# GEGLU feed-forward on one core: the place of ScalarE's Gelu table load, and of one token tile's second product in the down projection

## The chip, the core and the metric

The kernel runs on one core of a Trainium2 chip. TensorE multiplies matrices (PE in the profile, its weight loads are PEld), VectorE (DVE) and ScalarE (ACT) do elementwise work and move results between PSUM and SBUF, GpSimd (POOL) does some elementwise work, and SyncE (SP) issues most DMAs; ScalarE issues a few at the start. The metric is the device time in microseconds (us) of one execution. The five runs before the change gave 272.87 to 273.47 us, with a median of 273.18.

## What is computed

```python
B, S, D, F = 32, 32, 1024, 3584
x: (B, S, D)   w_gate, w_up: (D, F)   w_down: (F, D)      # all bfloat16

def reference(x, w_gate, w_up, w_down):
    return (_gelu(x @ w_gate) * (x @ w_up)) @ w_down      # gelu with the tanh approximation
```

There are 1024 tokens. The hidden tensor has 3584 columns, which is 28 tiles of 128.

## The kernel before

**How the program is written.** Every operation is recorded by one helper (`add`, line 52), so the profile names line 117, where all of them are emitted. Groups are told apart by the tiles that they write and read. TensorE runs its work in the order in which it is recorded. The other engines' operations, DMA issues among them, are sorted by a due time `at` and, where that is equal, by the order of recording (line 88). The due times are constants and running sums of expected matmul times; they order the queues and make nobody wait. Waits come from data: an operation waits for the writers and readers of the cells that it touches. Each engine works through its queue in order, so an operation that waits holds up all that stands behind it on that engine.

**The start (lines 196 to 230, and 247 to 270).** The first four column tiles of the hidden tensor are computed for the first 512 tokens, gate and up, in eight PSUM banks. The contraction over D goes by eight blocks k of 128. For k = 0 and 1, the tokens come in as they are (`xn`) and TensorE transposes them. For k = 2 to 7, they come in by transposing DMAs on SP's queue, the first of which (k = 2) stands behind SP's `xn` and its two gate loads. The weights `first` come in by block: SP loads gate of k = 0 and 1; ScalarE's queue holds half of `xn`, up of k = 0 and 1, then gate and up of k = 2, gate and up of k = 3 (lines 219 to 221), and then a one-column Gelu (line 222, into `warm`). That Gelu makes ScalarE load its table of functions early, long before the first Gelu that counts. All of these have the due time 0, so ScalarE takes them in the order of recording. The weights of k = 4 and 5, and of 6 and 7, also stand on ScalarE's queue, but the first of each waits for matmuls of k = 0 or of k = 1 (lines 264 to 267). After k = 3 the eight banks are copied to SBUF (`kept`).

**The up stage.** The hidden tensor is made with a seven-product block scheme in place of eight products: the two halves of the tokens by pairs of column tiles (p, p + 14), with sums of blocks of x in `S` and sums of weights in `T`. ScalarE and VectorE copy, apply Gelu and multiply, into `hT`.

**The down stage (lines 459 to 588).** The same scheme is used for `hT` times `w_down`: four token tiles t, halves of tokens, of contraction, and of output columns. Products are swept in the order 1, 2, 7, 5, 6, 3, 4 (line 491). A sweep has, for each of four token tiles, 14 matmuls (`NK`) of 512 columns; products 1 and 2 are in bfloat16, straight from `hT` and `w_down`, and the others take sums that VectorE and ScalarE prepare during the sweeps (`prep7` to `prep4`). A sweep accumulates in four PSUM banks, `PA` = 0 to 3 or `PB` = 4 to 7, one for each token tile. After product 1 of a token tile, ScalarE copies the bank of `PA` to one of `PB` (`done1`), since product 1 enters both the first output quarter and the others. Product 2 is then added to `PA`, which completes the output quarter (first tokens, first columns); `done2` copies it to `o11`, from where SP stores it.

One of these 28 sweeps over a token tile is placed differently. Sweep 2 goes over three token tiles only, by `range(5 - n)` on line 509. For the fourth, `done1` makes a second copy of product 1 into an SBUF tile `p1`. After sweep 4, at the very end, `p1` is put back into two banks, as 384 and 128 columns, and product 2 of this token tile is added there: 14 matmuls of 384 columns, then 14 of 128 (lines 578 to 588). ScalarE copies out the first piece and VectorE the second, and SP stores each. The start times `begin[n]` on lines 490 to 494 and the token tile that is held back to the end of the first four contraction steps (`held`, line 504) follow from this placement.

**The end.** Output DMAs have one due time, `end`, so SP takes them in the order of recording. SP then waits until all have landed.

Of the kernel before, what the change touches and what calls it, by code (L numbers as in the profile page):

```python
# [6 lines left out]
P = 128  # L7
BF16 = mybir.dt.bfloat16
FP32 = mybir.dt.float32
# [114 lines left out]
def bass_standalone__geglu_ffn__sampling_kernel(  # L124
# [10 lines left out]
    _, F = w_gate.shape  # L135
# [3 lines left out]
    out_r = of.rearrange("(tc p) d -> p tc d", p=P)  # L139
# [4 lines left out]
    pr = _Program()  # L144

    with ExitStack() as es:
        def sb(name, shape, dtype):
            return es.enter_context(nc.sbuf_tensor(name, shape, dtype))
# [6 lines left out]
        o11 = sb("o11", [P, 4, 512], BF16)  # L155
        ident = sb("ident", [P, P], BF16)
        warm = sb("warm", [P, 2], FP32)
        p1 = sb("p1", [P, 512], FP32)
        ps = es.enter_context(nc.psum_tensor("ps", [P, 8, 512], FP32))
        const0 = nc.const_aps.tensor(0.0, [P, 1], FP32)  # L160

# [3 lines left out]
        wd = [[arena[:, a:a + 7168].rearrange("p (k n) -> p k n", n=512) for a in row] for row in ((0, 7168), (14336, 21504))]  # L165
# [13 lines left out]
        def mm(bank, lhsT, rhs, start, stop, held=False, add=False):  # L179
            return pr.add("pe", held_matmul if held else "matmul", ps[:, bank, 0:rhs.shape[-1]], lhsT, rhs,  # L180
                          start=start, stop=stop, skip_group_check=add)
# [4 lines left out]
        def act(out, a, f, at):  # L186
            return pr.add("act", "activation", out, a, f, at=at)

        def dma(eng, out, a, at, name, after=()):
            return pr.add(eng, "dma_start", out, a, at=at, dma=name, after=after)  # L190

        GELU, COPY = ACTF.Gelu_apprx_tanh, ACTF.Copy
# [14 lines left out]
        def load_first(eng, j, k0, k1, after=()):  # L207
            dma(eng, first[:, j, k0:k1, :], w_r[j][:, k0:k1, 0:4 * P], 0, f"w0_{j}_{k0}", after)
# [10 lines left out]
        for k in range(2, 4):  # L219
            load_first("act", 0, k, k + 1)  # L220
            load_first("act", 1, k, k + 1)
        act(warm[:, 0:1], const0, GELU, 0)
        for k in range(NX):
            for i, b in enumerate((6, 7) if k == 0 else (4, 5)):
                half = ps[:, b, 0:P].bitcast(BF16)
# [22 lines left out]
        bank = lambda b: ps[:, b, :]  # L248
        steps = [(m, j, k) for k in range(DK - KO) for j in range(2) for m in range(4)]
        for m in range(4):  # L250
            steps += [(m, j, k) for j in range(2) for k in range(DK - KO, DK)] + [(m, None, None)]
        for m, j, k in steps:
            if j is None:
                at = 17.0 + m * 0.87
# [80 lines left out]
        def stat(p, j, k):  # L335
            if p in (8, 9):
                return brief[:, j, k, (p % 2) * P:(p % 2 + 1) * P]
            return pair_w(p, 0, slice(k, k + 1))[:, j, 0, :]

        for p in range(4, EARLY):  # L340
            at = 18.9 + (p - 4) * 3.46
# [23 lines left out]
        for p in range(NP):  # L365
# [11 lines left out]
            at = lambda s: t0 + s * SLOT  # L377
# [82 lines left out]
        NK = len(KL)  # L460
# [7 lines left out]
        def ht(i, j, k, t):  # L468
            m = (KL if j == 0 else KR)[k]
            return hT[:, m, i * 512 + t * P:i * 512 + (t + 1) * P]  # L470
# [13 lines left out]
        PA, PB = (0, 1, 2, 3), (4, 5, 6, 7)  # L484
# [3 lines left out]
        F, H = 0.2266, 0.216  # L488
        begin = {}
        now = base  # L490
        for n in (1, 2, 7, 5, 6, 3, 4):
            begin[n] = now
            now += (3 if n == 2 else 4) * NK * (H if n < 3 else F)
        end = now + NK * H

        def out_dma(i, t, j, src):
            dma("sp", out_r[:, 4 * i + t, j * 512:(j + 1) * 512], src, end, "out")
# [1 line left out]
        EDGE = 4  # L499

        def sweep(n, banks, start, stat, mov, done, prep=None):


            held = 2 if n == 7 else 3
            steps = [(t, k) for k in range(EDGE) for t in range(4) if t != held] + [(held, k) for k in range(EDGE)]
            steps += [(t, k) for k in range(EDGE, NK - EDGE) for t in range(4)]
            steps += [(t, k) for t in range(4) for k in range(NK - EDGE, NK)]
            if n < 3:
                steps = [(t, k) for t in range(5 - n) for k in range(NK)]
            made = set()  # L510
            for i, (t, k) in enumerate(steps):
                if prep and k // 2 not in made:
                    made.add(k // 2)
                    prep(k)
                mm(banks[t], stat(k, t), mov(k), start and k == 0, k == NK - 1, add=not start)
                if k == NK - 1:
                    done(t, begin[n] + (i + 1) * (H if n < 3 else F))

        def done1(t, at):
            act(bank(PB[t]), bank(PA[t]), COPY, at)  # L520
            if t == 3:
                act(p1[:, :], bank(PA[t]), COPY, at)
        sweep(1, PA, True, lambda k, t: ht(0, 0, k, t), lambda k: wd[0][0][:, k, :], done1)

        def done2(t, at):
            act(o11[:, t, :], bank(PA[t]), COPY, at)
            out_dma(0, t, 0, o11[:, t, :])
        sweep(2, PA, False, lambda k, t: ht(0, 1, k, t), lambda k: wd[1][0][:, k, :], done2)


# [34 lines left out]
        one_t = lambda b: (lambda k, t: S[:, s_at(b, k), t * P:(t + 1) * P])  # L565
        one_w = lambda b: (lambda k: T2r[:, t_at(b, k), :])
        sweep(7, PA, True, one_t(0), one_w(0), lambda t, at: act(p7[t], bank(PA[t]), COPY, at), prep7)
        sweep(5, PA, True, one_t(1), one_w(1), lambda t, at: act(p5[t], bank(PA[t]), COPY, at), prep5)
        sweep(6, PB, False, one_t(2), one_w(2), lambda t, at: act(bank(PA[t]), bank(PB[t]), COPY, at), prep6)
# [4 lines left out]
        sweep(3, PB, False, one_t(2), lambda k: S[:, c_at(0, k), :], done3, prep3)  # L574
        sweep(4, PA, False, lambda k, t: S[:, c_at(1, k), t * P:(t + 1) * P], one_w(2), done4, prep4)


        pieces = ((PB[0], 0, 384), (PB[1], 384, 512))
        for b, c0, c1 in pieces:
            act(ps[:, b, 0:c1 - c0], p1[:, c0:c1], COPY, begin[4] + 6)  # L580
        for b, c0, c1 in pieces:
            for k in range(NK):
                mm(b, ht(0, 1, k, 3), wd[1][0][:, k, c0:c1], False, k == NK - 1, add=True)
            if c0 == 0:
                act(o11[:, 3, c0:c1], ps[:, b, 0:c1 - c0], COPY, end)
            else:
                pr.add("dve", "tensor_copy", o11[:, 3, c0:c1], ps[:, b, 0:c1 - c0], at=end)
            dma("sp", out_r[:, 3, c0:c1], o11[:, 3, c0:c1], end, "out")

        sems, totals = pr.finish(nc, es)  # L590
        with nc.Block() as block:
            for name, e in (("sync", "sp"), ("scalar", "act"), ("gpsimd", "pool"), ("tensor", "pe"), ("vector", "dve")):
# [30 lines left out]
```

## Time and profile before

| | |
|---|---|
| median of five runs | 273.18 us (272.87 to 273.47) |
| the profiled execution | 273.33 us, of which the profile's span is 271.3 us |
| PE busy | 267.9 us, 99% of the span |
| DVE busy | 203.5 us, 75% |
| ACT busy | 132.8 us, 49% |
| POOL busy | 37.1 us, 14% |
| granted TensorE clock | 1.000 over the span |

The page gives each engine's busy time, then the span in 40 slices, the chain of work that ended last, and the costliest groups of instructions. In a group, "out<-in" names the tiles, and the last columns are the busy time, the mean duration of one instruction and the engine's idle time before them. The timeline gives start and length of merged runs of like instructions, in us from the start of the span; a "q" behind an engine's name (ACTq, SPq) is its instruction sequencer, which issues DMAs. Matmuls overlap: one of 512 columns in bfloat16 is shown with 0.38 us, but a new one starts every 0.216 us.

### The profile page before, as it was taken

How to read it: one execution, taken by the hardware profiler on the slowest of the kernel's cores; microseconds unless marked ns; L12 is line 12 of the kernel's file. 1: busy time of each engine (PE TensorE's matmuls, PEld its weight loads, DVE VectorE, ACT ScalarE, POOL GpSimd, SP SyncE). 2: the span in 40 equal slices, each digit the busy share in tenths (PEclk: the TensorE clock that was granted, in tenths of full speed). 3: DMA queues.
4: the chain of work that ended last, by engine and by line, in shares of the span. 5: the costliest groups of instructions: out<-in, count | busy, mean ns of one | idle time of the engine just before them, and what ended most of it. 6: DMA issues, size and time to landing. Idle time of an engine off the chain costs nothing.

```text
span 271.3 us, 3323 instructions
## 1 busy us (share of the span) xinstructions
PE 267.9 (99%) x1206; PEld 191.6 (71%) x1206; DVE 203.5 (75%) x238; ACT 132.8 (49%) x213; POOL 37.1 (14%) x23
## 2 busy tenths in 40 slices
PE   8999999999999999999999999999999999999996
PEld 3444448888888888888776776664458888888884
DVE  1341988898899889988764739289976999999911
ACT  2335777566756675667455564531220305067452
POOL 1000003023302330234345160000000000000000
PEclk9999999999999999999999999999999999999999
DMA  7999970050491500842900070293010000002102
GB/s 180 262 291 197 272 192 4 7 149 0 126 293 48 155 0 2 255 171 66 247 0 0 0 257 16 79 347 118 0 39 19 4 0 0 0 0 80 58 19 97
DMA packets 47039, 27.46 MB, mean 101 GB/s; under 512 B 8624, under 2 KB 47024, under 8 KB 47024
## 3 DMA queue, kind: packets, MB, share of 16 engines
q1 hardware_dynamic: 44800, 25.30, 34.2%
q10 hardware_dynamic: 2224, 1.97, 2.9%
q8 instruction: 9, 0.15, 0.2%
q14 instruction: 6, 0.05, 0.1%
HBM read 23.33 MB, written 2.10 MB: 94 GB/s over the span
## 4 chain that ended last, share of the span: by engine, by line
PE 96%; DMA 2%; SPq 0%; issue 0%; DVE 0%
PE ps L117 96%; DMA arena<-in_x_dram 2%; SPq L117 0%; DVE o L117 0%
## 5 line engine op out<-in xcount | busy, mean ns | idle before, releaser
L117 PE MATMUL ps<-S,T 128*128 128x512 f32 x560 | 129.2, 391 | 0.0
L117 PEld LDWEIGHTS ps<-S,T 128*128 128x128 f32 x560 | 105.1, 188 | 22.4
L117 ACT ACTIVATE tmp<-ps 128x512 f32<-128x512 f32 x64 | 37.9, 594 | 52.2 <-PE ps L117 52.2
L117 POOL TENSOR_TENSOR T<-arena 128x1024 fp32r<-128x1024 bf16 x17 | 36.4, 2151 | 124.6 <-PE ps L117 74.3
L117 PE MATMUL ps<-T,S 128*128 128x512 f32 x224 | 51.3, 390 | 0.0
L117 DVE TENSOR_TENSOR T<-arena,T 128x1024 fp32r<-128x1024 bf16 x42 | 50.9, 1218 | 0.2
L117 PEld LDWEIGHTS ps<-T,S 128*128 128x128 f32 x224 | 42.1, 188 | 8.8
L117 DVE TENSOR_TENSOR hT<-tmp,ps 128x512 bf16<-128x512 f32 x56 | 37.1, 684 | 14.3 <-PE ps L117 11.9
L117 PE MATMUL ps<-arena 128*128 128x512 bf16 x192 | 43.2, 382 | 0.4 <-DMA arena<-in_x_dram 0.3
L117 ACT ACTIVATE ps<-ps 128x512 f32<-128x512 f32 x44 | 25.6, 584 | 36.6 <-PE ps L117 36.6
L117 DVE TENSOR_TENSOR tmp<-ps,tmp 128x512 f32<-128x512 f32 x28 | 19.4, 691 | 23.2 <-PE ps L117 23.2
L117 PEld LDWEIGHTS ps<-arena 128*128 128x128 bf16 x192 | 17.7, 98 | 24.5 <-issue 3.8
L117 DVE TENSOR_TENSOR T<-arena 128x1024 fp32r<-128x1024 bf16 x25 | 30.0, 1218 | 5.0 <-PE ps L117 4.4
L117 PE MATMUL ps<-arena,hT 128*128 128x512 bf16 (+2 forms) x126 | 24.6, 356 | 0.0
L117 DVE TENSOR_TENSOR ps<-ps,tmp 128x512 f32<-128x512 f32 x32 | 22.2, 695 | 3.0 <-PE ps L117 3.0
L117 PEld LDWEIGHTS ps<-arena,hT 128*128 128x128 bf16 x126 | 11.7, 98 | 12.7 <-issue 0.5
L117 ACT ACTIVATE tmp<-tmp 128x512 f32<-128x512 f32 x28 | 17.6, 631 | 2.4 <-DVE tmp L117 2.1
L117 DVE TENSOR_TENSOR S<-hT 128x1024 fp32r<-128x1024 bf16 x14 | 16.6, 1217 | 0.0
L117 ACT ACTIVATE T<-arena 128x1024 fp32r<-128x1024 bf16 x14 | 14.8, 1060 | 0.0
L117 ACT ACTIVATE ps<-hT 128x512 f32<-128x512 f32 x18 | 10.7, 599 | 8.0 <-DVE hT L117 8.0
L117 ACT ACTIVATE hT<-ps 128x512 f32<-128x512 f32 x14 | 8.0, 599 | 10.9 <-PE ps L117 10.9
L117 PE MATMUL ps<-S 128*128 128x512 f32 x56 | 12.9, 389 | 0.0
(32 smaller groups left out, 88.8 us busy)
## 6 DMA issues: line engine op xcount, KB each, us to landing
arena<-in_w_down_dram SPq DMA_DIRECT2D x4, 1792.0 KB, 9.3
arena<-in_w_gate_dram SPq DMA_DIRECT2D x10, 512.0 KB, 3.9
arena<-in_w_up_dram SPq DMA_DIRECT2D x10, 512.0 KB, 6.0
out_dram<-arena SPq DMA_DIRECT2D x12, 128.0 KB, 1.7
arena<-in_w_gate_dram SPq DMA_DIRECT2D x4, 256.0 KB, 5.0
arena<-in_w_up_dram SPq DMA_DIRECT2D x4, 256.0 KB, 5.2
arena<-in_w_up_dram ACTq DMA_DIRECT2D x4, 128.0 KB, 4.8
arena<-in_w_gate_dram ACTq DMA_DIRECT2D x2, 256.0 KB, 5.0
```

The costliest lines, as they stand in the source:

```text
L117: ins = name(eng, *args, **kw) if callable(name) else getattr(eng, name)(*args, **kw)
```

## The change

Two things change. First, the one-column Gelu on `warm` moves forward on ScalarE's queue by two DMA issues: it now stands behind gate and up of k = 2 and ahead of gate and up of k = 3. Second, the late placement of the fourth token tile's product 2 is taken out: sweep 2 covers all four token tiles, `p1`, its copies, the two pieces and their stores are gone, and the fourth token tile of this quarter is copied to `o11` and stored in `done2` as the other three are. The bookkeeping of `begin`, `end` and `held` follows.

```diff
-        p1 = sb("p1", [P, 512], FP32)
...
         for k in range(2, 4):
             load_first("act", 0, k, k + 1)
             load_first("act", 1, k, k + 1)
-        act(warm[:, 0:1], const0, GELU, 0)
+            if k == 2:
+                act(warm[:, 0:1], const0, GELU, 0)
...
         for n in (1, 2, 7, 5, 6, 3, 4):
             begin[n] = now
-            now += (3 if n == 2 else 4) * NK * (H if n < 3 else F)
-        end = now + NK * H
+            now += 4 * NK * (H if n < 3 else F)
+        end = now
...
-            held = 2 if n == 7 else 3
-            steps = [(t, k) for k in range(EDGE) for t in range(4) if t != held] + [(held, k) for k in range(EDGE)]
+            steps = [(t, k) for k in range(EDGE) for t in range(3)] + [(3, k) for k in range(EDGE)]
...
             if n < 3:
-                steps = [(t, k) for t in range(5 - n) for k in range(NK)]
+                steps = [(t, k) for t in range(4) for k in range(NK)]
...
-        def done1(t, at):
-            act(bank(PB[t]), bank(PA[t]), COPY, at)
-            if t == 3:
-                act(p1[:, :], bank(PA[t]), COPY, at)
-        sweep(1, PA, True, lambda k, t: ht(0, 0, k, t), lambda k: wd[0][0][:, k, :], done1)
+        sweep(1, PA, True, lambda k, t: ht(0, 0, k, t), lambda k: wd[0][0][:, k, :],
+              lambda t, at: act(bank(PB[t]), bank(PA[t]), COPY, at))
...
-        pieces = ((PB[0], 0, 384), (PB[1], 384, 512))
-        for b, c0, c1 in pieces:
-            act(ps[:, b, 0:c1 - c0], p1[:, c0:c1], COPY, begin[4] + 6)
-        for b, c0, c1 in pieces:
-            for k in range(NK):
-                mm(b, ht(0, 1, k, 3), wd[1][0][:, k, c0:c1], False, k == NK - 1, add=True)
-            if c0 == 0:
-                act(o11[:, 3, c0:c1], ps[:, b, 0:c1 - c0], COPY, end)
-            else:
-                pr.add("dve", "tensor_copy", o11[:, 3, c0:c1], ps[:, b, 0:c1 - c0], at=end)
-            dma("sp", out_r[:, 3, c0:c1], o11[:, 3, c0:c1], end, "out")
```

## The prediction

> **What bounds the kernel now.** I read the page's busy times first, then the chain that ended last, then the timelines of both ends, because the change touches the first 12 us and the last sweeps.
>
> ```profile
> span 271.3 us, 3323 instructions
> PE 267.9 (99%) x1206; PEld 191.6 (71%) x1206; DVE 203.5 (75%) x238; ACT 132.8 (49%) x213; POOL 37.1 (14%) x23
> PE 96%; DMA 2%; SPq 0%; issue 0%; DVE 0%
> ```
>
> TensorE is busy all the time. So only three things can move the end: TensorE's own work, a hole in its stream, and what comes before its first or after its last matmul. The chain in order of time shows them:
>
> ```profile
> 2.22 6.62 DMA arena<-in_x_dram
> ...
> 8.97 260.11 PE ps L117 x1174
> ...
> 269.11 0.29 DVE o L117
> ```
>
> The one wait at the front is for a transposing DMA of x, the slice of k = 2, issued at 2.22. From 8.97 on, TensorE never waits until VectorE's last copy. TensorE's timeline gives the prices:
>
> ```profile
> 4.61 4.03 PE L117 MATMUL ps<-arena 128*128 128x512 bf16 x16
> 8.97 13.40 PE L117 MATMUL ps<-arena 128*128 128x512 bf16 x61 [0.33 <-DMA arena<-in_x_dram]
> ...
> 181.19 21.32 PE L117 MATMUL ps<-arena,hT 128*128 128x512 bf16 x98
> 202.17 38.44 PE L117 MATMUL ps<-T,S 128*128 128x512 f32 x168
> 240.45 12.86 PE L117 MATMUL ps<-S 128*128 128x512 f32 x56
> 253.14 12.85 PE L117 MATMUL ps<-T,S 128*128 128x512 f32 x56
> 265.84 3.23 PE L117 MATMUL ps<-arena,hT 128*128 128x384 bf16 x28
> ```
>
> The 98 matmuls are sweeps 1 and 2 (56 + 42). They start every (21.32 - 0.38) / 97 = 0.216 us, 0.38 being the length shown of the last one. The last row is the piece that the change removes.
>
> ScalarE's timeline at the start, where each weight load is one row:
>
> ```profile
> 2.28 0.45 ACTq L117 DMA_DIRECT2D arena<-in_w_gate_dram  x1
> 2.76 0.45 ACTq L117 DMA_DIRECT2D arena<-in_w_up_dram  x1
> 3.24 0.45 ACTq L117 DMA_DIRECT2D arena<-in_w_gate_dram  x1
> 3.73 0.47 ACTq L117 DMA_DIRECT2D arena<-in_w_up_dram  x1
> 4.23 1.28 ACT L117 ACT_TABLE_LOAD   x1 [4.23 <-issue]
> 5.52 0.20 ACT L117 ACTIVATE warm<-const-float32-0.0 128x1 f32<-128x1 f32 x1
> 6.95 0.39 ACTq L117 DMA_DIRECT2D arena<-in_w_gate_dram  x1
> ```
>
> **Part 1, the down projection.** *TensorE.* 14 matmuls of 512 columns come into sweep 2: 14 x 0.216 = 3.02 us. All later sweeps move back by that. The last sweep (4) ended at 253.14 + 12.85 = 265.99, so TensorE now ends at 269.01. Before, it ended at 265.84 + 3.23 = 269.07. Gain 0.06.
>
> *The tail behind the last matmul.* Before: VectorE copies 128 columns in 0.29 us and a store of 32 KB lands 1.44 us after issue. After: the last token tile of sweep 4 has an odd number, so ScalarE copies 512 columns and 128 KB are stored. Both stood in the trace already, only not last: that copy ran at 266.03 for 0.60 us, 0.04 behind its matmul, and its store landed in 1.70 us.
>
> ```profile
> 266.03 0.60 ACT L117 ACTIVATE arena<-ps 128x512 bf16<-128x512 f32 x1 [1.22 <-PE ps L117]
> 268.32 0.49 ACT L117 ACTIVATE o<-ps 128x384 bf16<-128x384 f32 x1 [1.69 <-PE ps L117]
> ```
>
> So the copy costs 0.60 - 0.29 = 0.31 more and the store 1.70 - 1.44 = 0.26 more. SP's final wait and the engines' exits follow the landing alike. **Sum of part 1: -0.06 + 0.31 + 0.26 = +0.51 us.** The rows are close copies of what will run, so I allow 0.1 either way.
>
> *What else moves.* Gone from ScalarE: the copy to `p1` (0.59 us) and two copies back (0.47 and 0.26), all beside TensorE's work; gain nothing. Added: one copy to `o11` (0.60 us) at the end of sweep 2. It frees the fourth bank for sweep 7, which holds that token tile back by 12 matmuls (2.7 us), so 2.1 us are spare; without that cover it would cost 0.64. Its store joins SP's queue behind three like it and lands in 1.7 us; the next store behind it is due some 40 us later. VectorE is the risk: it is busy 47.8 of the 51 us from 203 to 254. But it prepared sweep 7 by 201.5 and then stood still for 4.35 us until sweep 7 released a buffer at 205.8. With sweep 7 3.02 us later, that wait is 3.02 longer and all behind it keeps its distance to TensorE, which had no hole there. Due times of `prep3` and `prep4` shift by up to 3.02 too, and VectorE's order stays. Cost nothing; were VectorE to lose one preparation (1.22 us) of its lead, at most that.
>
> **Part 2, the table load.** Nothing is added: 1.28 us of load and 0.20 us of Gelu move ahead of two issues. GpSimd's queue is not touched, and SP's only by the store above. The first Gelu that counts is due at about 17 us, so neither place matters for it. What counts is whether the two issues are held. In the trace's records, VectorE's semaphore instructions in its busiest stretch come about 0.13 us after the start of the instruction before them, not earlier: a sequencer seems to hand over an instruction only as the engine starts it. By that, gate of k = 3 is issued when `warm` starts: 3.24 + 1.28 = about 4.55 in place of 3.24, and up of k = 3 at 5.05 in place of 3.73. The ends are 0 and 1.28 + 0.20 = 1.5 us; I take 1.3.
>
> *Is that late?* Gate landed at 8.58 and was first needed at 8.97 + 8 x 0.216 = 10.70; up landed at 9.78 and was needed at 11.56. Slack 2.12 and 1.78. A shift of 1.3 to 1.5 is covered. The loads behind them wait for k = 0 until 6.95, when ScalarE is free either way (up of k = 3 is issued by 5.7).
>
> *Does anything gain?* The k = 2 slice of x, issued at 2.22, landed at 8.84; 15 of the 16 DMA engines had reported by 8.10, the last 0.74 later, while that engine set was also moving the weights of k = 3 (their packets run from 6.58 to 9.1). Held weights leave that stretch to x. TensorE, from 8.26 on (its sixteenth matmul of k = 0 and 1), could have gone on at 8.48, and went on at 8.97. So the gain lies between 0 and 0.49. Contention could also turn against x, by the loads meeting the later slices instead; k = 3's slice landed at 10.10 for a need at 10.70, so a loss needs 0.6 first. I take 0.30: the laggard near the other engines, not fully.
>
> [...]
>
> **The sum.** +0.51 - 0.30 = +0.2 us. The profiled execution took 273.33, 0.15 above the median, so 273.5 against it, and 273.4 as a median. About 0.2% (0.55 us) is what a measurement of this kernel can tell from no change.
>
> **The rivals.** *A, the issues are not held, or x comes no earlier.* For it: the data of that slice had all started moving by 6.95, and up to 6.57 ScalarE's ring is full of k = 2 whatever happens. Against: the one late DMA engine. It gives +0.51, 273.7, just inside 0.2%.
>
> *B, slower: the weights of k = 3 come late.* Moved back, they stand behind or beside the transposes that SP issues at 3.49 and 4.78. The slowest issue of that time, a transpose at 7.39, took 6.8 us to land. If up of k = 3, issued at 5.2, took that, it would land at 12.0; with x 0.30 earlier it is needed at 11.26, so TensorE stands for 0.74, and the sum is +0.51 - 0.30 + 0.74 = +0.95, 274.1. It decides as soon as up of k = 3 lands over 0.35 late. Against: ScalarE's loads took 4.5 to 6.1 us, and 5.2 + 6.1 = 11.3.
>
> *C, no cost at the end and the full slot at the front.* The stores' landing could be as short as the 1.44 of 32 KB: -0.06 + 0.31 - 0.49 = -0.24, 272.9. Even this isn't faster by 0.2%; that needs 0.3 us more, which no row offers.
>
> **How the numbers follow.** Forecast (x earlier by 0.1 to 0.49, the tail as computed, 273.1 to 273.7): 0.55. A: 0.25. B: 0.12. C: 0.05; something I don't see: 0.03. The range leaves out the far part of B and C and the unseen: 272.95 to 274.05. Slower by over 0.2%: 0.03 of the forecast, four tenths of A as its centre lies 0.04 us from the bound (0.10), nearly all of B (0.11), 0.01 unseen: 0.25. Faster: 0.03. Within 0.2%: 0.72.
>
> **What would show it.** In ScalarE's timeline, the table load should start near 3.2 and gate of k = 3 be issued near 4.55; if it is issued near 3.3, A holds. TensorE's rows at the start should part at 8.5 to 8.8 in place of 8.97, and have no new wait near 10.5 to 11.6 (B). There should be one run of 112 matmuls for sweeps 1 and 2, no hole after it, and the last instruction should be ScalarE's copy of 0.60, with a 128 KB store behind it. A wait of TensorE in sweeps 5 or 6 would mean that VectorE's lead was thinner than I read it.

## The result, and the profile after

The changed kernel takes 273.77 us (median of 33 runs, 273.06 to 274.76); the kernel before, measured beside it, 272.97 (56 runs, 272.27 to 274.25). The ratio is 1.0028 with a 95% interval of 1.0020 to 1.0036: slower by 0.76 us, 0.55 to 0.98. The forecast was 273.4 in a range of 272.95 to 274.05, with +0.2 us against before. The range holds the time, but the loss is larger than forecast, and one term of the sum was wrong.

The page of the changed kernel, then its chain in order of time (start, length, what):

```profile
span 272.0 us, 3290 instructions
PE 268.4 (99%) x1192; PEld 190.9 (70%) x1192; DVE 203.2 (75%) x237; ACT 131.8 (48%) x210; POOL 37.2 (14%) x23
PE 99%; ACT 0%; issue 0%
```

```profile
0.73 0.04 issue
0.78 3.88 PE ps L117 x16
4.66 0.05 issue
4.71 264.51 PE ps L117 x1176
269.22 0.02 issue
269.24 0.60 ACT arena L117
```

The chain no longer passes through a DMA: in this execution TensorE waits for nothing from 4.71 on. And yet the span is longer, 271.96 us in place of 271.27 in the traces' records. TensorE's timeline at both ends:

```profile
4.71 20.65 PE L117 MATMUL ps<-arena 128*128 128x512 bf16 x90
...
181.37 24.35 PE L117 MATMUL ps<-arena,hT 128*128 128x512 bf16 x112
205.36 38.46 PE L117 MATMUL ps<-T,S 128*128 128x512 f32 x168
243.66 12.86 PE L117 MATMUL ps<-S 128*128 128x512 f32 x56
256.35 12.85 PE L117 MATMUL ps<-T,S 128*128 128x512 f32 x56
```

Sweeps 1 and 2 are one run of 112 matmuls, the later sweeps stand unbroken behind it, and sweep 4 ends at 256.35 + 12.85 = 269.20. ScalarE's timeline at the end and at the start:

```profile
269.24 0.60 ACT L117 ACTIVATE arena<-ps 128x512 bf16<-128x512 f32 x1 [1.22 <-PE ps L117]
```

```profile
2.76 0.45 ACTq L117 DMA_DIRECT2D arena<-in_w_up_dram  x1
3.25 1.28 ACT L117 ACT_TABLE_LOAD   x1 [3.25 <-issue]
3.31 0.39 ACTq L117 DMA_DIRECT2D arena<-in_w_gate_dram  x1
3.73 0.48 ACTq L117 DMA_DIRECT2D arena<-in_w_up_dram  x1
4.54 0.20 ACT L117 ACTIVATE warm<-const-float32-0.0 128x1 f32<-128x1 f32 x1
7.62 0.42 ACTq L117 DMA_DIRECT2D arena<-in_w_gate_dram  x1
```

The last lines decide the second half of the change. The table load starts at 3.25 and runs to 4.53, but gate of k = 3 is issued at 3.31, while it runs, and up of k = 3 at 3.73, as before. The one-column Gelu takes its turn on the engine at 4.54, after both. So the issues are not held; the queue goes on past a running table load and past a Gelu that has not begun.

**Where the 0.69 us between the two traces lie.** I cut both at TensorE's first matmul on `S` and `T`, which is the first one of the seven-product scheme: at 40.02 us before and 40.19 after, so the start took 0.17 more. From there to the last matmul it is 228.84 before and 228.63 after, 0.21 less. From the last matmul's start to the span's end it is 2.42 before and 3.15 after, 0.73 more. Together +0.69. The last store is a different one in each; the first row is that of before, the second that of the changed kernel (size, median us from issue to landing):

```profile
out_dram<-o SPq DMA_DIRECT2D x1, 32.0 KB, 1.4
```

```profile
out_dram<-arena SPq DMA_DIRECT2D x12, 128.0 KB, 1.7
```

### The profile page after: what moved, and what is told of

Same layout as the page of the kernel before. It is cut to its first block, busy times and chain, and to the rows that moved or that the text cites. A ratio compares the mean times of both kernels' runs of the same rounds, so it can differ in the third digit from the quotient of the medians.

```text
span 272.0 us, 3290 instructions
## 1 busy us (share of the span) xinstructions
PE 268.4 (99%) x1192; PEld 190.9 (70%) x1192; DVE 203.2 (75%) x237; ACT 131.8 (48%) x210; POOL 37.2 (14%) x23
## 4 chain that ended last, share of the span: by engine, by line
PE 99%; ACT 0%; issue 0%
PE ps L117 99%; ACT arena L117 0%
## 5 line engine op out<-in xcount | busy, mean ns | idle before, releaser
L117 PE MATMUL ps<-arena,hT 128*128 128x512 bf16 x112 | 24.3, 379 | 0.0
L117 PEld LDWEIGHTS ps<-arena,hT 128*128 128x128 bf16 x112 | 10.9, 98 | 13.3 <-issue 0.3
```

Source lines behind the costliest of these rows:

```text
L117: ins = name(eng, *args, **kw) if callable(name) else getattr(eng, name)(*args, **kw)
```

## The experiments

There were two questions: whether the loss comes from the end alone, or whether the moved table load costs something at the start that one trace can't show; and whether the forecast's gain at the start would have come, had the weights really been held. Each ratio is to the kernel before, run beside it. Three kernels, e8_nowarm, e9_half and e10_eighth, were run once each, for their traces alone.

### The table load alone, and the end alone

e1_table, the kernel before with only the first part of the diff:

```diff
-        act(warm[:, 0:1], const0, GELU, 0)
+            if k == 2:
+                act(warm[:, 0:1], const0, GELU, 0)
```

> The kernel before with the table load moved alone; its late product is kept. Theory 1 (the 0.52 us at the end that both traces show is not all: the moved table load makes the start dearer on average): 0.15 to 0.35 us slower than before. Theory 2 (the load doesn't hold the issues, so the start is the same but for chance): within 0.1 us of before. The forecast's own step (the issues are held and x of k = 2 comes earlier): 0.1 to 0.4 us faster. In the profile, the two gate and up issues of k = 3 near 3.31 and 3.73 by theories 1 and 2.

Measured: ratio 1.0004 (0.9988 to 1.0019). ScalarE's timeline has the load at 3.25, the two issues at 3.31 and 3.73 and the Gelu at 4.54, as in the changed kernel. The slices of x landed no earlier (8.94 us for k = 2, against 8.84 before).

e2_tail, the kernel before with only the second part of the diff:

```diff
-            now += (3 if n == 2 else 4) * NK * (H if n < 3 else F)
-        end = now + NK * H
+            now += 4 * NK * (H if n < 3 else F)
+        end = now
...
-        pieces = ((PB[0], 0, 384), (PB[1], 384, 512))
```

> The kernel before with product 2 of the fourth token tile back in its sweep; the table load stays behind k = 3. Theory 1: 0.45 to 0.6 us slower than before, less than the whole change. Theory 2: as slow as the whole change, 0.55 to 0.95 us, which the end alone would then have to give (only 0.52 is in the traces). From the last matmul's start to the end of the span 3.15 us in place of 2.42, by both.

Measured: ratio 1.0009 (0.9994 to 1.0024). The end is as expected, 3.15 us. The whole times of these two kernels can't tell the theories apart: the interval of a ratio over some dozen runs is 0.8 us wide.

### What the whole times can't tell, the records can

Cut at the first matmul on `S` and `T`, the traces fall into two parts of very different kind:

| kernel | product 2 of the fourth tile | first matmul on S and T | from there to the end |
|---|---|---|---|
| before | late, 384 + 128 | 40.02 | 231.25 |
| e1_table | late, 384 + 128 | 40.12 | 231.27 |
| e3_held | late, 384 + 128 | 39.33 | 231.27 |
| e5_held_again | late, 384 + 128 | 39.24 | 231.29 |
| e7_x_first | late, 384 + 128 | 42.25 | 231.24 |
| e11_table_first | late, 384 + 128 | 39.97 | 231.28 |
| after | in sweep 2 | 40.19 | 231.77 |
| e2_tail | in sweep 2 | 39.46 | 231.80 |
| e6_after_held | in sweep 2 | 40.31 | 231.76 |
| e8_nowarm | in sweep 2 | 39.29 | 231.78 |
| e4_whole | late, 512 | 40.82 | 231.82 |
| e9_half | late, 256 + 256 | 39.80 | 231.55 |
| e12_eighth_apart | late, 448 + 64 | 39.67 | 231.62 |
| e10_eighth | late, 448 + 64, with a wait (below) | 40.29 | 233.11 |

The last column repeats to within 0.05 us and depends on the end alone: 231.27 in the mean with the small last piece, 231.78 in the mean of the four with product 2 in its sweep. So the second part of the change costs 0.51 us, shown by ten traces. The column before it moves by 1.5 us (39.29 to 40.82) even without the three held kernels and e7_x_first, among kernels whose early instructions hardly differ. That is the noise of this kernel. Where the table load moved forward without a hold (after, e1_table, e11_table_first) the column has 40.19, 40.12 and 39.97; where it stayed (before, e2_tail, e4_whole, e9_half, e10_eighth, e12_eighth_apart) it has 40.01 in the mean, from 39.46 to 40.82.

### What the end is made of

e4_whole keeps the late place and takes away the small piece:

```diff
-        pieces = ((PB[0], 0, 384), (PB[1], 384, 512))
+        pieces = ((PB[0], 0, 512),)
```

> The kernel before with the late product 2 kept late but in one piece of 512 columns, not 384 and 128. If the gain of the late placement lies only in the small last piece (copy of 0.29 in place of 0.60 us, store of 1.44 in place of 1.70): 0.5 us slower than before, from the last matmul's start to the end of the span about 2.95 us (0.17 less than with an fp32 last matmul). If it lies in the place itself (relief for VectorE or the banks in between): no more than 0.2 us slower.

Measured: ratio 1.0029 (1.0015 to 1.0043), and 231.82 us in the table, as slow as with product 2 in its sweep. From the last matmul to the end it is 3.15, not 2.95 as I wrote, because a bfloat16 matmul of 512 columns, shown with 0.38 us, ends no earlier than the fp32 one with 0.39. The place itself buys nothing; only the small last piece does. ScalarE's last copy in this kernel:

```profile
269.91 0.60 ACT L117 ACTIVATE o<-ps 128x512 bf16<-128x512 f32 x1 [2.44 <-PE ps L117]
```

e9_half, e10_eighth and e12_eighth_apart change the size of the last piece.

```diff
+        pieces = ((PB[0], 0, 256), (PB[1], 256, 512))      # e9_half
+        pieces = ((PB[0], 0, 448), (PB[1], 448, 512))      # e10_eighth
```

> The kernel before with the late product in pieces of 256 and 256 columns in place of 384 and 128. By the forecast's sum of the end: matmuls 14 x 2 x 0.109 = 3.05 us, as before; VectorE's last copy of 256 columns about 0.42 in place of 0.29, by the rows of 128 and 512 columns (0.29, 0.69); the store of 64 KB about 1.50 in place of 1.44; from TensorE's first matmul of k = 4 to the end of the span 259.03 us, 0.2 more than before (258.84). If the size of the last piece doesn't matter and only its being apart does: 258.85.

Measured: 231.55 from the first matmul on `S` and `T`, 0.28 more than with 128 columns (0.2 was expected). The copy took 0.43 and the store 1.56. The size of the last piece is what counts.

```profile
268.93 0.43 DVE L117 CAST o<-ps 128x256 bf16<-128x256 f32 x1 [3.29 <-PE ps L117]
```

> The kernel before with the late product in pieces of 448 and 64 columns. If a matmul of 64 columns starts every 0.028 us, as half of one of 128: the copy takes about 0.23 in place of 0.29 and the store about 1.42, and from k = 4 to the end it is 0.05 to 0.1 us less than before (258.75). If the weight load of 0.1 us sets the pace instead: 14 x 0.03 to 0.07 us more, 0.35 to 0.9 us more than before (259.2 to 259.7).

Measured: matmuls of 64 columns start every 0.029 us, so the weight load (98 ns each in the profile of before) doesn't set the pace. But the end came 1.84 us later than with 128. VectorE's row tells why:

```profile
271.33 0.22 DVE L117 CAST o<-ps 128x64 bf16<-128x64 f32 x1 [5.22 <-DMA out_dram<-o]
```

It waited for the store of the first piece. The program tracks SBUF in cells of 256 bytes; column 448 lies inside a cell that the first piece's store reads. This was a fault of the experiment, so the last 64 columns got a tile of their own:

```diff
+        tip = sb("tip", [P, 64], BF16)
...
-                pr.add("dve", "tensor_copy", o11[:, 3, c0:c1], ps[:, b, 0:c1 - c0], at=end)
+                pr.add("dve", "tensor_copy", tip[:, :], ps[:, b, 0:c1 - c0], at=end)
```

> The kernel before with pieces of 448 and 64 columns again, the last 64 columns now in an SBUF tile of their own, so that VectorE's copy no longer waits for the store of the first piece (in the run before it waited 1.9 us for that). From TensorE's first matmul on S and T to the end of the span: 231.27 us for the kernel before; here the copy 0.22 in place of 0.29, the store 1.41 in place of 1.44, the matmuls 14 x (0.189 + 0.029) = 3.05 as before, so 231.15, 0.1 us less. In the time of whole runs this is below what rounds can tell: ratio 0.998 to 1.001. If the store of the first piece, issued at most 0.5 us earlier, holds up the last one on SP's queue: 0.2 to 0.4 us more than before.

Measured: ratio 1.0002 (0.9988 to 1.0015); 231.62 in the table, 0.35 more than before. The copy did shorten, but the store didn't come earlier, and it took 1.53 us to land in place of 1.44. SP's timeline at the end:

```profile
268.98 0.33 SPq L117 DMA_DIRECT2D out_dram<-o  x1
269.35 0.43 SPq L117 DMA_DIRECT2D out_dram<-tip  x1
```

ScalarE's copy of 448 columns ends at 268.95, so SP issues that store at 268.98 and is ready for the next only at 269.35, 0.31 after VectorE's copy of the 64 columns had ended (268.81 + 0.23 = 269.04). The 384 and 128 of the kernel before are the best of the sizes tried: a last piece of 256 or 512 columns costs more by itself, and with 64 the first store is in the way, which it isn't with 128 (issued at 268.84, for a last copy that ends at 269.40).

### Really holding the weights

e3_held makes the issue of k = 3's weights wait for the Gelu to end, in the kernel before:

```diff
+        warmed = act(warm[:, 0:1], const0, GELU, 0)
+        load_first("act", 0, 3, 4, [warmed])
+        load_first("act", 1, 3, 4)
```

> The kernel before with the table load ahead of the weights of k = 3, and the issue of these made to wait until the one-column Gelu has ended, so that they are really held: gate issued near 4.8 in place of 3.24. By the forecast's step the k = 2 slice of x then lands earlier and nothing is late: 0.1 to 0.5 us faster than before. Rival B of the forecast: up of k = 3 lands after 11.5 and TensorE waits there: 0.3 to 0.8 us slower. If x's landing is set by what is already in the queues at 4.8 (k = 2's weights and x itself): within 0.1.

Measured: ratio 0.9991 (0.9975 to 1.0008). Now the issues are held:

```profile
4.54 0.20 ACT L117 ACTIVATE warm<-const-float32-0.0 128x1 f32<-128x1 f32 x1
4.77 0.35 ACTq L117 DMA_DIRECT2D arena<-in_w_gate_dram  x1
5.15 0.46 ACTq L117 DMA_DIRECT2D arena<-in_w_up_dram  x1
```

The k = 2 slice of x landed at 8.15, the k = 3 slice at 8.61 (10.10 before), and the held weights landed at 9.10 and 9.99, in time. That fits DMA engines that gave their time to x, but it is one trace. The same kernel again:

> The kernel of the run with the held weights of k = 3 once more, on another chip or at another time, since its first interval (0.9975 to 1.0008) doesn't tell a gain of 0.3 us from none. Theory H (held weights leave the DMA engines to x, whose k = 2 and 3 slices come earlier): the two together give a ratio near 0.999, 0.2 to 0.4 us faster than before, and the k = 3 slice of x lands near 8.6 again (9.7 to 11.4 where the weights weren't held). Theory 0 (the fast looks were chance): ratio within 0.0005 of 1, and that slice lands anywhere from 8.6 to 11.

Measured: ratio 1.0012 (0.9994 to 1.0030), with those slices at 7.31 and 7.65 in its trace. The k = 3 slice landed at 7.65 to 8.93 in the three kernels that only hold the weights (with e6_after_held, below), and at 8.95 to 11.37 in the ten that hold nothing: it does come earlier, by no fixed amount. The k = 2 slice, for which TensorE waits first, landed at 7.31 to 8.15 with the hold, inside the 7.04 to 9.33 of the ten. The two ratios, one below 1 and one above, show no gain in time; the second interval leaves room for 0.16 us. The changed kernel with held weights, which is what the forecast took the change to be:

> The changed kernel with the weights of k = 3 made to wait for the one-column Gelu, so that it does what the forecast took it to do. Theory H: 0.52 us lost at the end and 0.2 to 0.4 gained at the start, 0.1 to 0.35 us slower than before. Theory 0: 0.5 us slower than before, as the change itself.

Measured: ratio 1.0023 (1.0004 to 1.0042), 0.63 us, nearer to the 0.5 of no gain. Its trace has a further wait in TensorE's timeline:

```profile
13.56 1.69 PE L117 MATMUL ps<-arena 128*128 128x512 bf16 x7 [0.31 <-DMA arena<-in_w_up_dram]
```

The up weights of k = 4 and 5, one load, are late there (landed 13.52). This load is on ScalarE's queue behind a wait for k = 0's matmuls, which ended late in this execution, so gate and up were issued at 7.25 and 7.66 in place of 6.95 and 7.37. That need not be a price of the hold: in e10_eighth, which holds nothing, the same load was issued late too (7.93), landed at 13.50, and the matmul that needs it began 0.20 us late.

e7_x_first keeps the hold and pushes further: SP hands the gate weights of k = 1 to ScalarE's queue, so that x goes out 0.47 us earlier.

```diff
-            load_first("sp", 0, k, k + 1)
+            load_first("act" if k else "sp", 0, k, k + 1)
```

> The kernel before with held weights of k = 3 and, further, the gate weights of k = 1 moved from SP's queue to ScalarE's, ahead of up of k = 1, so that SP issues the k = 2 slice of x 0.45 us earlier. If TensorE's start is set by that slice: it lands 0.3 to 0.5 us earlier, near 7.7, and the kernel is 0.2 to 0.6 us faster than before. If gate of k = 1 then comes late (it is needed at 6.4 to 7, and landed at 5.96 from SP): a new wait of up to 0.5 us there, and no gain over the held kernel. Where TensorE's clock rises late, neither shows.

Measured: ratio 1.0048 (1.0033 to 1.0064), 1.3 us slower. The slice, issued earlier, landed at 8.66, later than with the hold alone (8.15 and 7.31), and the weights came late one after another (up of k = 0 landed at 6.01, gate of k = 3 at 11.22, gate of k = 4 and 5 at 14.40; before, at 4.40, 8.58 and 11.55):

```profile
6.06 4.72 PE L117 MATMUL ps<-arena 128*128 128x512 bf16 x20 [0.45 <-DMA arena<-in_w_up_dram]
11.27 2.13 PE L117 MATMUL ps<-arena 128*128 128x512 bf16 x8 [0.49 <-DMA arena<-in_w_gate_dram]
14.45 0.82 PE L117 MATMUL ps<-arena 128*128 128x512 bf16 x3 [1.04 <-DMA arena<-in_w_gate_dram]
```

Here, sending one slice out earlier brought it no sooner, and these weights landed 1.61 to 2.85 us later than before.

### The place of the table load

e8_nowarm takes the one-column Gelu away; the table is then loaded where the first activations need it.

```diff
-            if k == 2:
-                act(warm[:, 0:1], const0, GELU, 0)
```

> The changed kernel without the one-column Gelu, so that the table is loaded just ahead of the first Gelu that counts. If the place of the load matters to nothing: ScalarE loads it while it waits for TensorE, and from TensorE's first matmul of k = 4 to the end of the span the time is that of the changed kernel, 259.36 us within 0.05. If it holds up the first Gelu: that Gelu starts up to 1.3 us later, and as the next tiles wait for its bank, up to 1.3 us are added.

Measured: 231.78 from the first matmul on `S` and `T`, as in the changed kernel, and 259.37 from the first matmul of k = 4. ScalarE's timeline:

```profile
9.53 1.28 ACT L117 ACT_TABLE_LOAD   x1 [9.53 <-PE ps L117]
10.82 2.07 ACT L117 ACTIVATE hT<-ps 128x512 f32<-128x512 f32 x4
12.90 1.28 ACT L117 ACT_TABLE_LOAD   x1
15.79 0.60 ACT L117 ACTIVATE tmp<-ps 128x512 f32<-128x512 f32 x1 [1.60 <-PE ps L117]
```

There are now two loads, one ahead of the first copies and one ahead of the first Gelu at 15.79. The second lies in time in which ScalarE waited for TensorE. The first holds up the copies a little: they begin 2.57 us behind TensorE's first matmul of k = 2 (8.25), in place of 2.14 before (11.11 - 8.97). The time from k = 4 on shows nothing of it. e11_table_first puts the Gelu, in the kernel before, ahead of all DMA issues.

```diff
+        act(warm[:, 0:1], const0, GELU, 0)
         NX = 2
         for i, eng in enumerate(("sp", "act")):
```

> The kernel before with the one-column Gelu, and so the table load, at the very front of ScalarE's queue, ahead of all DMA issues. If a table load and a Gelu are handed to the engine without holding the queue: the first DMA issue comes within 0.15 us of its 0.74, all others within 0.1 of theirs, and the time is within the noise of before (0.2 us either way). If the load holds the queue: every issue 1.3 us later, TensorE's start 1 us or more later, and over 0.8 us slower.

Measured: ratio 1.0012 (0.9991 to 1.0032); each of the seven issues that wait for nothing stays within 0.1 us of its place; the first rows are:

```profile
0.73 1.28 ACT L117 ACT_TABLE_LOAD   x1 [0.73 <-PEq L608]
0.79 0.47 ACTq L117 DMA_DIRECT2D hT<-in_x_dram  x1
1.29 0.97 ACTq L117 DMA_DIRECT2D arena<-in_w_up_dram  x2
2.03 0.20 ACT L117 ACTIVATE warm<-const-float32-0.0 128x1 f32<-128x1 f32 x1
```

At the front, in the middle, behind k = 3 or left out: the load costs nothing that these runs can tell.

## Why the prediction was right or wrong, by its steps

**Part 1, +0.51 at the end: right, term by term.** From the first matmul on `S` and `T`, TensorE's stream shortened by 0.21 to the start of the last matmul and, as that one is longer by 0.17, by 0.04 to its end; 0.06 was forecast. The copy measured 0.60, the store 1.69. Ten traces give 0.51 for the sum. e4_whole and e9_half show that the size of the last piece is the cause and its late place is not.

**What was costed at nothing: right.** VectorE's wait before sweep 5 grew as forecast, from 4.35 to 7.39 us (3.02 more was forecast), and TensorE had no hole behind it:

```profile
209.02 1.22 DVE L117 TENSOR_TENSOR T<-arena 128x1024 fp32r<-128x1024 bf16 x1 [7.39 <-PE ps L117]
```

**Part 2, "gate of k = 3 is issued when `warm` starts": wrong, and it is the step that failed.** It was issued 0.06 us after the table load began. I had inferred from VectorE's semaphore instructions that a sequencer hands over an instruction only as the engine starts it. In e11_table_first three DMA issues begin (at 0.79 and from 1.29 on) while the table load runs, from 0.73 to 2.01, and the Gelu still stands behind it, to begin at 2.03. So ScalarE's queue went on there past two instructions, one that ran and one that had not begun. My records were of another engine and another kind of instruction; why they come no earlier there stays open. The measurement decides against my reading. The load itself took 1.28 us in the timelines above, and the instruction behind it that had its data ready began 0.01 to 0.02 us after its end.

**"I take 0.30" for an earlier x: wrong twice.** First, the weights were not held, so there was no reason for it (rival A's mechanism, and its +0.51). Second, where I did hold them, the k = 2 slice came within its usual scatter, and the whole time showed no gain: 0.9991 and 1.0012. The forecast priced x alone. TensorE's start has two more conditions, its clock and the other loads, and the last section has their numbers.

**The range and the chances.** The range holds the time because it was wide enough for rival A: A's sum, 273.7, is what came (273.77), and not the 273.4 that the forecast's own step gives. As far as the forecast's mechanism goes, that is luck. The forecast put 0.72 on a change within 0.2% and 0.25 on a slower one; the ratio is 0.28%, with 0.20% as the lower end of its interval, so the less likely of the two came.

**Rival B** (weights of k = 3 late, 0.95 us slower) didn't happen in the changed kernel; its pattern, gate of k = 3 late and TensorE waiting for it, is what e7_x_first shows. **Rival C** is ruled out by the last column of the table: the end costs 0.51, where C has 0.25.

**What stays open.** The end gives 0.51 us, and the measured loss is 0.76 with a lower bound of 0.55. The two kernels that share this end and not the table load, e2_tail and e4_whole, gave 1.0009 and 1.0029, on both sides of 0.51 us (1.0019), and the table load alone gave 1.0004. The kernel before itself had a median of 272.97 beside the changed kernel and of 273.13 to 273.32 in the four later rounds, which is a shift of the size that is missing. I take the remaining quarter of a microsecond for chance of the start, since the only issue there that the change moved is gate of k = 3, by 0.07 us, and the starts in the table don't part by the place of the load. That is argued and not shown.

## What to carry to other kernels

In a kernel whose main engine never waits, what lies behind the last matmul can be added up from rows that already stand in the trace (here 0.51 us, forecast and measured). A small last piece shortened the copy and the store here (0.29 and 1.44 us with 128 columns, 0.60 and 1.69 with 512), as long as the store before it was off the queue by then: with 64 columns it wasn't, and the end came 0.35 us later than with 128. Where an instruction stands on an engine's queue can say little about when the issues behind it go out (here one went out 0.06 us after the table load ahead of it had begun): look for an issue that passes a running instruction, or make one wait, before pricing a hold. If whole times scatter by more than the effect, cut the traces at a landmark behind the noisy stretch and compare the parts.

## What the hardware showed that I hadn't expected

**The clock at the start rose at no fixed time, which cost up to 1 us.** In the matmul records of before, matmuls of 512 columns start every 0.427 us at first and every 0.216 later; the trace's clock records begin full speed at 5.49 us. In the changed kernel it is 6.74, and over the 12 traces that have such a record, 3.47 to 6.74, in no order that the edits would give. The 16 matmuls of k = 0 and 1 took 4.44 us in the changed kernel and 3.45 in e5_held_again, where all ran at full speed. The windows of before, then of the changed kernel, count the matmuls of two stretches of 2 us (stretch, its length, PE busy and number, granted clock, DMA share, GB/s):

```profile
4.80:6.80 2.00, 2.00 (x9) 1.00 1.13 215
6.80:8.80 2.00, 1.84 (x9) 1.00 1.19 177
```

```profile
4.80:6.80 2.00, 2.00 (x6) 1.00 1.11 257
6.80:8.80 2.00, 2.00 (x11) 1.00 1.20 199
```

Six matmuls in place of nine in the first: the slice of x landed early there (7.76), and TensorE, still slow, was not ready for it before 9.1. The view's own clock column reads 1.00 in both; only the counts tell. The record of full speed lasts 266.24 us in seven of the 12 traces and 269.65 in the other five, two lengths that lie 3.41 us apart. What sets its start, no run shows.

**The landing of one early DMA moves by over 2 us.** The k = 2 slice of x was issued between 2.22 and 2.23 us in all kernels but e7_x_first, and landed between 7.04 and 9.33. TensorE's third block begins at the later of that landing and its own readiness: at 8.97 before, behind a landing at 8.84, and at 9.14 in the changed kernel, where the slice landed at 7.76 and the matmuls of k = 0 and 1 filled the time to then. In the ten kernels that hold nothing, it begins between 8.25 and 9.47. So these two, the clock and the landing, make 1.2 us of the 1.5 us by which the table's start moves. The rest comes from like waits behind it: TensorE stood 0.31 us for the k = 3 slice in e4_whole and 0.23 in e11_table_first, and 0.20 for weights in e10_eighth. Whole runs of before differ by 2.0 us (272.27 to 274.25).
